# Loads of u, v and z that wait for a matmul of PE, and an earlier turn of u of group 3, in a fused gated-attention and maxout kernel

## The chip, the cores and the metric

The kernel runs on one core of a Trainium2 chip. The metric is the device time of one execution in microseconds. Five engines work side by side, each with an instruction queue of its own: PE (matrix multiplications), DVE and ACT (elementwise work), POOL and SP (in this kernel almost only issuers of DMA transfers; POOL also does a few copies at the start). An instruction that has to wait holds up everything behind it in its own queue[...]. The transfers that they issue share 16 DMA engines.

## The reference

Eight sequences of 3072 rows. For each one a gate over squared-ReLU attention is computed, and its rows then go through a maxout feed-forward:

```python
scores = (1.0 / S) * np.matmul(z, z.transpose(0, 2, 1))   # z: 8 x 3072 x 64
attn = np.maximum(scores, 0.0) ** 2
x = (u * np.matmul(attn, v)).reshape(B * S, D)            # u, v: 8 x 3072 x 256
g = np.maximum(x @ w1, x @ w2)                            # w1, w2: 256 x 1024
out = g @ w_out                                           # w_out: 1024 x 256
```

Inputs and output are float32 in memory; the kernel multiplies in bfloat16.

## The kernel before

**Tiling.** A sequence (batch b) has 24 tiles of 128 rows. Four tiles make a group (6 per batch, g = 0 to 5), eight tiles a piece (3 per batch), two groups a couple (3 per batch, c = 0 to 2). A block A(g, blk) holds the squared scores between two groups as 128 x 2048 bfloat16; 28 such blocks are at hand and are handed round. The scores are symmetric, so about half of the blocks are computed (`score_pair`: two matmuls into PSUM at L220, ReLU on ACT at L233 into r_sb, of which there are three, and the square on DVE at L239 or L241). The others are transposes of these, made by a DMA transpose on SP (`mirror`, L272; the blocks on the diagonal are filled up by small transposes at L244). mirror(b, g, blk) gives A(blk, g).

**Stages.** Batch 0's first four groups are worked one after the other (i = 0 to 3, slots with the tile number n; matmuls at L288). From there on the loop over couples runs (i = 2 is couple (0,2), i = 3 is (1,0), and so on to i = 23). A couple has a list of steps, each with two matmuls on half of PE's rows (L905). Couple (0,2) is "plain", with 96 steps; the others multiply by a Strassen-like scheme with 84 steps, for which DVE makes sums and differences of blocks (`prepare`: L340, L344, L348, and L797 in the couple) and of v (`combine_v`: L174 to L177). Score pairs of blocks that are wanted later are spread between the steps. After a couple's steps comes `second`, the feed-forward of the couple before it: two calls of `ff` (L450, L464, L473), with the outputs copied by ACT (L485) and written out by DMAs that POOL issues (L486). While PE is in `second`, DVE works through a list of tasks for the next couple: the gates (`gate`, L434: attention output times turned u), the combinations of v, the sums and differences.

**Loads.** POOL issues the loads of u, v and z, which turn float32 into bfloat16 on the way. `load_u` (L190) fetches one group of u in two transfers of 128 KB (of bfloat16); there are two buffers, and a buffer is free when `turn_u` has read it. `turn_u` (L196) is a DMA transpose on SP that gives uT, also two buffers, read by the gates. `load_z` (L136) fetches a piece of z; `turn_z` copies it twice on DVE (L143) and transposes it on SP (L144) into zT, from which the score pairs read. `load_v` (L160) fetches a piece of v or a part of it; there are five buffers.

**What sets the order.** The order of each queue is written out by hand. In the couples, `plan` lists (step, what to do): at that step of the loop the instruction is put into its engine's queue. For a DMA on POOL this is a place in POOL's queue only: when POOL gets there, the transfer leaves as soon as its buffer is free, whatever step PE is at. In batch 0, SP's queue has around group 3 (i = 3): mirrors (0,3,4) and (0,0,5) at n = 0; mirror (0,1,5) and then `turn_z(1, 1)` at n = 4; mirror (0,3,5) at n = 8; `turn_u(0, 3)` at n = 13; `turn_z(1, 2)` at n = 17; then u of groups 4 and 5 at steps 1 and 4 of couple (0,2). POOL's queue has the load of u of group 3 at n = 1, then the first feed-forward's outputs (group 0), loads of u of groups 4 and 5, group 1's outputs, and then the v loads of couple (0,2). The gates of group 3 are the first DVE tasks of the feed-forward that follows.

In the plain couple (0,2) pieces of v are taken in the order 2, 1, 0. The second of them begins at step 32 with A(5,2) and takes A(5,3), which mirror (0,3,5) makes, from step 36 on. Its seventh score pair, at step 27, is the first that reads the z tiles of `turn_z(1, 1)`. At the end of the last couple of a batch, `load_v(b + 1, 0)` is put into POOL's queue (the buffer is that of v piece 2 of batch b); `combine_v` of that piece is the third of three in DVE's list.

The lines that the change turns on, apart from those in the diff:

```python
if b and b + 1 < B and c == 2:
    load_v(b + 1, 0)
if i + 1 < len(couples):
    forms, tasks = prepared(i + 1, gates)
```

Of the kernel before, what the change touches and what calls it, by code (L numbers as in the profile page):

```python
# [11 lines left out]
def kernel(  # L12
# [10 lines left out]
    nc = tc.nc  # L23
# [12 lines left out]
    G = 4  # L36
# [7 lines left out]
    AFTER = mybir.DependencyInfo(mybir.DependencyClass.Sync, mybir.DependencyReason.DATA)  # L44
# [23 lines left out]
    def by_tile(x):  # L68
        return x.rearrange("(p t) d -> p t d", t=NT)
# [29 lines left out]

    zT = zpool.tile([P, 4 * 2 * G, P], bf16, name="zT", bufs=1)
    zn, zd, z_first = {}, {}, []

# [27 lines left out]
    def load_z(b, piece, held=False):  # L132
        zn[b, piece] = zpool.tile([P, 2 * G, dqk], bf16, name="zn")
        if held:
            nc.vector.memset(zn[b, piece][:, 0, 0:1], 0.0)
        nc.gpsimd.dma_start(  # L136
            out=zn[b, piece], in_=by_tile(z[b])[:, ds(piece * 2 * G, 2 * G), :]
        )

    def turn_z(b, piece):  # L140
        t = zpool.tile([P, 2 * G, 2, dqk], bf16, name="zd")
# [10 lines left out]
    def load_v(b, piece, lo=0, n=2 * G, held=False):  # L152
        if (b, piece) not in vp:
            vp[b, piece] = vpool.tile([P, 2 * G, D], bf16, name="v_sb")
        t = vp[b, piece]
        if held:
            nc.vector.memset(t[:, lo, 0:1], 0.0)
        step = 2 if b > 1 else n
        for k in range(lo, lo + n, step):
            nc.gpsimd.dma_start(  # L160
                out=t[:, ds(k, step), :], in_=by_tile(v[b])[:, ds(piece * 2 * G + k, step), :]
            )

    def v_at(b, t, dc):
        return vp[b, t // (2 * G)][:, t % (2 * G), ts(dc, P)]
# [16 lines left out]
    un, uT = {}, {}  # L182

    def load_u(b, g, held=False):
        un[b, g] = unat.tile([P, G, D], bf16, name="un")
        if held:
            nc.vector.memset(un[b, g][:, 0, 0:1], 0.0)
        step = 2 if b or g > 1 else G
        for k in range(0, G, step):
            nc.gpsimd.dma_start(  # L190
                out=un[b, g][:, ds(k, step), :], in_=by_tile(u[b])[:, ds(g * G + k, step), :]
            )

    def turn_u(b, g):
        t = upool.tile([P, G, KD, P], bf16, name="uT")
# [368 lines left out]
    with tc.manual_schedule():  # L564
# [49 lines left out]
        for i in range(PLAIN):  # L614
            b, g = groups[i]
            if i:
                acc = new_acc()
            new, slots = {}, pair_slots(i)
            for slot, (n, dc) in enumerate(steps_of(i)):
                tick += 1  # L620
                k = need(b, g, n)
                upto = max(k, min(done + 1, k + AHEAD)) if slot in slots else k
                while done < min(upto, len(pairs)):
                    emit_pair()
                if i == 0 and slot in (10, 22):
                    zT_pe(12 if slot == 10 else 20, 8 if slot == 10 else 4, "act")
                    if slot == 22:
                        for x in z_first:
                            x.release()
                attn_unit(b, g, n, acc, dc, n == 0, n == NT - 1)  # L630
                if n == NT - 1 and i < PLAIN - 1:
                    if i < 2:
                        new[dc] = drain_fast(acc, dc)
                    else:
                        new.update(drain(acc, [dc]))
                if dc:
                    continue
                if i in (1, 2) and n in (5, 8):
                    k = n // 8
                    nc.vector.tensor_add(sums[k][0], *sums[k])  # L640
                    sums[k] = sums[k][0]
                first = 17 if i == 3 else 11
                if i and n == first:
                    gates = gate(*groups[i - 1], sums)
                if i and n in (first, first + 3):
                    gates.pop(0)()
                if i == 0 and n == 14:
                    turn_u(0, 0)
                if (i, n) in ((1, 8), (2, 1), (3, 1)):
                    load_u(0, i, held=True)  # L650
                if i and n == (0, 16, 14, 13)[i]:
                    turn_u(0, i)
                if (i, n) in ((0, 18), (2, 12)):
                    w_in = ((w2_sb, moe_w2), (w1_sb, moe_w1)) if i == 0 else ((w_out_sb, moe_w_out),)
                    nc.vector.memset(w_in[0][0][:, 0, 0:1], 0.0)
                    for w_sb, w in w_in:
                        nc.gpsimd.dma_start(
                            out=w_sb, in_=w.rearrange("(c p) f -> p c f", p=P)
                        )
                if later and n % 4 == 0 and (i == 3 or i and n > 12):  # L660
                    later.sort(key=lambda block: block[2])
                    mirror(*later.pop(0))
                if i == 2 and n == 16:
                    nc.vector.tensor_sub(w15_sb, w1_sb, w2_sb)  # L664
                    w1.release()
                    w2.release(after=COOL)
                if (i, n) == (2, 15):
                    nc.sync.dma_start_transpose(
                        w2T.ap.rearrange("p (k r) -> p k r", r=P), w2.ap
                    )  # L670
                if (i, n) in ((1, 16), (2, 14)):
                    load_z(1, i - 1, held=True)
                if (i, n) in ((2, 17), (3, 4)):
                    turn_z(1, i - 2)
                if (i, n) == (3, 5):
                    load_z(1, 2, held=True)
                if (i, n) == (3, 17):
                    turn_z(1, 2)
            sums = new
# [65 lines left out]
        b, g = groups[PLAIN - 1]  # L745
# [9 lines left out]
        for i in range(PLAIN // 2, len(couples)):  # L755
            b, c = couples[i]
# [3 lines left out]
                b, c, forms, supers=PLAIN_COUPLES.get(i)  # L760
# [78 lines left out]
            plan = [(1, turn_u, b, q1), (4, turn_u, b, q2)]  # L839
            if i + 1 < len(couples):  # L840
                nb, nc_ = couples[i + 1]
                plan += [(70, load_u, nb, 2 * nc_), (76, load_u, nb, 2 * nc_ + 1)]
            if b + 1 < B:
                plan += (
                    [
                        (8, load_z, b + 1, 0),
                        (14, load_z, b + 1, 1),
                        (44, turn_z, b + 1, 0),
                        (58, turn_z, b + 1, 1),
                    ],  # L850
                    [(8, load_z, b + 1, 2), (44, turn_z, b + 1, 2), (45, load_v, b + 1, 2)],
                    [(10, load_v, b + 1, 1)],
                )[c]
            if i == 2:
                plan = [
                    (1, turn_u, 0, 4),
                    (4, turn_u, 0, 5),
                    *((17 + 8 * k, load_v, 1, (1, 2, 0)[k // 2], k % 2 * G, G) for k in range(6)),
                ]
            if i == 3:  # L860
                plan = [
                    (2, load_u, 1, 0),
                    (6, load_u, 1, 1),
                    (14, load_z, 2, 0),
                    (18, load_z, 2, 1),
                    (22, turn_u, 1, 0),
                    (26, turn_u, 1, 1),
                    (66, turn_z, 2, 0),
                    (len(steps), load_u, 1, 2),
                    (len(steps), load_u, 1, 3),  # L870
                ]
# [11 lines left out]
            for s, pair in enumerate(steps):  # L883
                while halves_done and halves_done[0][0] <= s:
                    _, name, mm = halves_done.pop(0)
# [13 lines left out]
                for half, (name, w, blk, j) in enumerate(pair):  # L899
                    rows = ds(half * R, R)  # L900
                    if name not in acc:
                        acc[name] = acc_tile((PLAIN_BANK if plain else BANK)[name])
                    a = blk()
                    left[name] -= 1
                    mm = nc.tensor.matmul(  # L905
                        a.out(acc[name]),
                        w()[rows],
                        a.moving(rows, j),
                        start=name not in opened,
                        stop=left[name] == 0,  # L910
                    )
                    opened[name] = True
                    if (s, half) in marks:
                        halves_done.append((s + (2 if plain else G), marks[s, half], mm))
                    if (s, half) in waits:
                        relay = relays[waits[s, half]]
                        tc.add_manual_dep(mm.ins, relay.ins.name, AFTER, reason="half done")
                    a.quota -= 1
                    if not a.quota:
                        a.release()  # L920
# [48 lines left out]
```

## Time and profile before

| what | value |
|---|---|
| median of 14 runs | 916.36 us |
| lowest, highest | 914.9, 921.52 us |
| the profiled execution: its time, its span | 914.9 us, 913.1 us |
| mean granted TensorE clock | 0.998 |
| share of the span in the chain that ended last | PE 96%, DVE 1%, ACT 1%, the rest under 1% each |
| DMA: SP's queue (transposes for the most part) | 359040 packets, 91.79 MB, 62.6% of 16 engines' span |
| DMA: POOL's queue (loads and outputs) | 37424 packets, 52.58 MB, 32.1% |
| POOL idle ahead of outputs (L486), for ACT's copies | 535.1 us, 86 times |
| POOL idle ahead of loads of u (L190), for turns of u | 89.6 us, 13 times |
| POOL idle ahead of loads of v (L160), for matmuls | 27.2 us, 7 times |

How to read it. The span is one execution, from the first to the last instruction; the 1.8 us between it and the execution's time lie around it. In the chain of waits the profile goes back from the last instruction, at each step to what released it; an engine with 96% of that chain has the work that sets the end. Idle time of POOL and SP says nothing by itself: they wait by design. In the timelines, a line gives start and duration in us, engine, line, operation, what is written and read, the count, and in brackets the idle time just before and what ended it. "SPq" marks SP's issuing of DMAs; its duration is the issue, not the transfer.

### The profile page before, as it was taken

The numbers are of one execution on the slowest core, as the hardware profiler recorded it, in microseconds if no ns is written. First come the engines' busy times: TensorE is split into PE (matmuls) and PEld (weight loads), VectorE is DVE, ScalarE is ACT, GpSimd is POOL, SyncE is SP. The second block draws the span as 40 slices with busy tenths as digits, with TensorE's granted clock in tenths as the row PEclk, the third lists the DMA queues.
The fourth block names the chain that finished last, engine by engine and source line by source line (L and its number), as shares of the span: only waits on it lengthen the run. The fifth ranks groups of instructions, "written<-read, shape, count | busy, mean of one in ns | idle before, by whom it ended". The sixth has DMA issues, their size and how long they took to land.

```text
span 913.1 us, 19389 instructions
## 1 busy us (share of the span) xinstructions
PE 899.3 (98%) x7478; PEld 520.8 (57%) x7526; DVE 722.5 (79%) x1097; ACT 601.4 (66%) x1192; POOL 160.8 (18%) x303
## 2 busy tenths in 40 slices
PE   9998999999999999999999999999999999999998
PEld 4454565665565655665546656566465564655655
DVE  6753689788997799887997979979799788995640
ACT  7985967567666676667666666766766667673445
POOL 4102021211202121201213022030320212101000
PEclk9999999999999999999999999999999999999999
DMA  9999999989999997999979999898988999887201
GB/s 176 166 191 187 175 187 166 177 153 162 184 178 161 171 174 124 186 161 166 188 128 200 147 166 181 139 210 149 164 165 137 187 162 175 163 165 138 75 24 70
DMA packets 396557, 145.61 MB, mean 159 GB/s; under 512 B 361904, under 2 KB 387632, under 8 KB 396464
## 3 DMA queue, kind: packets, MB, share of 16 engines
q1 hardware_dynamic: 359040, 91.79, 62.6%
q0 software_dynamic: 37424, 52.58, 32.1%
q8 instruction: 59, 0.97, 0.4%
q14 instruction: 34, 0.28, 0.1%
HBM read 59.77 MB, written 25.17 MB: 93 GB/s over the span
## 4 chain that ended last, share of the span: by engine, by line
PE 96%; DVE 1%; issue 1%; ACT 1%; DMA 0%; ACTq 0%; SPq 0%; DVEq 0%
PE acc L905 44%; PE o_ps L473 18%; PE d_ps L450 18%; PE s_ps L220 7%; PE o_ps L464 5%; PE acc L288 4%; ACT r_sb L233 1%; DVE blk L241 0%; DMA uT<-un 0%; PE acc L592 0%; DVE xT L434 0%; PE w2o_ps L686 0%; PE tpz L125 0%; DVE w_sb L664 0%; DVE blk L239 0%
## 5 line engine op out<-in xcount | busy, mean ns | idle before, releaser
L905 PE MATMUL acc<-blk,v_sb 64*128 64x512 bf16 x2208 | 453.2, 378 | 0.0
L233 ACT ACTIVATE r_sb<-s_ps 128x512 bf16<-128x512 f32 (+3 forms) x672 | 335.3, 560 | 126.2 <-PE s_ps L220 76.3
L905 PE MATMUL acc<-blk,vt 64*128 64x512 bf16 x1512 | 364.1, 376 | 0.0
L905 PEld LDWEIGHTS <-v_sb 64*128 64x128 bf16 x2208 | 179.0, 94 | 135.0 <-issue 7.7
L241 DVE TENSOR_TENSOR blk<-r_sb 128x1024 bf16<-128x1024 bf16 x257 | 172.2, 688 | 76.2 <-ACT r_sb L233 75.5
L457 ACT ACTIVATE g_sb<-d_ps 128x512 bf16<-128x512 f32 x384 | 193.4, 629 | 29.3 <-PE acc L905 17.8
L473 PE MATMUL o_ps<-w_out_sb,g_sb 128*128 128x256 bf16 x1536 | 175.5, 273 | 0.0
L905 PEld LDWEIGHTS <-vt 64*128 64x128 bf16 x1512 | 139.2, 94 | 62.3
L450 PE MATMUL d_ps<-xT,w_sb 128*128 128x512 bf16 x720 | 167.7, 379 | 2.6 <-issue 0.2
L473 PEld LDWEIGHTS <-g_sb 128*128 128x128 bf16 x1536 | 150.3, 98 | 17.4
L485 ACT COPY o_sb<-o_ps 128x512 f32<-128x512 f32 (+1 forms) x98 | 56.4, 577 | 132.9 <-PE o_ps L473 132.9
L486 POOL DMA_DIRECT2D out_dram<-o_sb x88 | 48.1, 547 | 535.1 <-ACT o_sb L485 535.1
L220 PE MATMUL s_ps<-zT 64*128 64x512 bf16 (+3 forms) x676 | 130.4, 358 | 4.6 <-ACT r_sb L233 4.1
L782 DVE TENSOR_TENSOR h_sb<-h_sb,acc 128x512 f32<-128x512 f32 x168 | 109.4, 682 | 28.7 <-ACT h_sb L786 20.9
L450 PEld LDWEIGHTS <-w_sb 128*128 128x128 bf16 x768 | 73.2, 98 | 89.4 <-issue 9.8
L344 DVE TENSOR_TENSOR blk<-blk,blk 128x2048 bf16<-128x2048 bf16 x63 | 77.2, 1225 | 4.5 <-DMA blk<-blk 2.4
L340 DVE TENSOR_TENSOR blk<-blk,blk 128x2048 bf16<-128x2048 bf16 x63 | 76.7, 1218 | 0.0
L797 DVE TENSOR_TENSOR blk<-blk,blk 128x2048 bf16<-128x2048 bf16 x63 | 76.6, 1218 | 0.0
L434 DVE SCALAR_TENSOR_TENSOR xT<-h_sb,uT 128x512 bf16<-128x512 f32 x96 | 62.0, 684 | 17.7 <-DMA uT<-un 16.4
L348 DVE TENSOR_TENSOR blk<-blk,blk 128x2048 bf16<-128x2048 bf16 x63 | 73.3, 1218 | 0.1
L190 POOL DMA_DIRECT2D un<-in_u_dram x94 | 50.4, 558 | 107.3 <-DMA uT<-un 89.6
L239 DVE TENSOR_TENSOR blk<-r_sb 128x512 bf16<-128x512 bf16 (+3 forms) x162 | 46.5, 324 | 20.0 <-ACT r_sb L233 18.9
(49 smaller groups left out, 358.1 us busy)
## 6 DMA issues: line engine op xcount, KB each, us to landing
out_dram<-o_sb POOLq DMA_DIRECT2D x88, 256.0 KB, 3.7
un<-in_u_dram POOLq DMA_DIRECT2D x92, 128.0 KB, 5.0
v_sb<-in_v_dram POOLq DMA_DIRECT2D x74, 128.0 KB, 5.3
blk<-blk SPq DMA_TRANSPOSE x240, 4.8
v_sb<-in_v_dram POOLq DMA_DIRECT2D x11, 256.0 KB, 7.3
zn<-in_z_dram POOLq DMA_DIRECT2D x21, 128.0 KB, 4.1
out_dram<-o_sb SPq DMA_DIRECT2D x6, 256.0 KB, 2.0
blk<-in_moe_w_dram POOLq DMA_DIRECT2D x2, 512.0 KB, 6.1
```

The source lines that it names most:

```text
L220: nc.tensor.matmul(s_ps[h][:, lo[h] :], zT[rows, z_at(b, blk * G + tiles[h]), :], zT[rows, q + lo[h] // P : q + G, :].rearrange("p t c -> ...
L233: nc.scalar.activation(o, s, AF.Relu)
L241: nc.vector.tensor_mul(a[:, k : k + 2, :], r, r)
L340: nc.vector.tensor_add(*alike(f["S1"], f["A21"], f["A22"]))
L344: nc.vector.tensor_sub(*alike(f["S2"], f["S1"], f["A11"]))
L348: nc.vector.tensor_sub(*alike(f["S3"], f["A11"], f["A21"]))
L450: nc.tensor.matmul(d_ps, w15_sb[:, kc, ts(nb, P)], xT[:, kc, :], start=(kc == 0), stop=(kc == KD - 1),)
L457: nc.scalar.activation(g_sb[:, nb, :], d_ps, AF.Relu)
L473: nc.tensor.matmul(o_ps[t // 2][:, t % 2, :], g_sb[:, nb, ts(t, P)], w_out_sb[:, nb, :], start=False, stop=(nb == KF - 1 and t % 2 == 1),)
L782: nc.vector.tensor_add(out, a, b_)
L797: nc.vector.tensor_sub(f["A12"].ap, f["A12"].ap, f["S2"].ap)
L905: mm = nc.tensor.matmul(a.out(acc[name]), w()[rows], a.moving(rows, j), start=name not in opened, stop=left[name] == 0,)
```

## The change

Every load of u, v and z in the loop over couples now waits for the matmul that stands last in PE's queue at the place where the load is put into POOL's queue (`pace` holds it; it is empty before the first couple, so that earlier loads don't wait). The places in `plan` are spread more widely, and loads of a whole piece of v are split in two. `turn_u(0, 3)` moves from n = 13 to n = 3 in group 3, that is, ahead of mirror (0,1,5), `turn_z(1, 1)` and mirror (0,3,5) in SP's queue. The load of v piece 0 after a batch's last couple keeps its place in the code, and waits there for that couple's last matmul.

```diff
--- before.py
+++ after.py
@@ -99,6 +99,15 @@
 
 
 
+    pace = []
+
+    def load(tile_, source):
+        dma = nc.gpsimd.dma_start(out=tile_, in_=source)
+        if pace:
+            tc.add_manual_dep(dma.ins, pace[-1].ins.name, AFTER, reason="paced")
+
+
+
     zT = zpool.tile([P, 4 * 2 * G, P], bf16, name="zT", bufs=1)
     zn, zd, z_first = {}, {}, []
 
@@ -133,9 +142,7 @@
         zn[b, piece] = zpool.tile([P, 2 * G, dqk], bf16, name="zn")
         if held:
             nc.vector.memset(zn[b, piece][:, 0, 0:1], 0.0)
-        nc.gpsimd.dma_start(
-            out=zn[b, piece], in_=by_tile(z[b])[:, ds(piece * 2 * G, 2 * G), :]
-        )
+        load(zn[b, piece], by_tile(z[b])[:, ds(piece * 2 * G, 2 * G), :])
 
     def turn_z(b, piece):
         t = zpool.tile([P, 2 * G, 2, dqk], bf16, name="zd")
@@ -157,9 +164,7 @@
             nc.vector.memset(t[:, lo, 0:1], 0.0)
         step = 2 if b > 1 else n
         for k in range(lo, lo + n, step):
-            nc.gpsimd.dma_start(
-                out=t[:, ds(k, step), :], in_=by_tile(v[b])[:, ds(piece * 2 * G + k, step), :]
-            )
+            load(t[:, ds(k, step), :], by_tile(v[b])[:, ds(piece * 2 * G + k, step), :])
 
     def v_at(b, t, dc):
         return vp[b, t // (2 * G)][:, t % (2 * G), ts(dc, P)]
@@ -187,9 +192,7 @@
             nc.vector.memset(un[b, g][:, 0, 0:1], 0.0)
         step = 2 if b or g > 1 else G
         for k in range(0, G, step):
-            nc.gpsimd.dma_start(
-                out=un[b, g][:, ds(k, step), :], in_=by_tile(u[b])[:, ds(g * G + k, step), :]
-            )
+            load(un[b, g][:, ds(k, step), :], by_tile(u[b])[:, ds(g * G + k, step), :])
 
     def turn_u(b, g):
         t = upool.tile([P, G, KD, P], bf16, name="uT")
@@ -648,7 +651,7 @@
                     turn_u(0, 0)
                 if (i, n) in ((1, 8), (2, 1), (3, 1)):
                     load_u(0, i, held=True)
-                if i and n == (0, 16, 14, 13)[i]:
+                if i and n == (0, 16, 14, 3)[i]:
                     turn_u(0, i)
                 if (i, n) in ((0, 18), (2, 12)):
                     w_in = ((w2_sb, moe_w2), (w1_sb, moe_w1)) if i == 0 else ((w_out_sb, moe_w_out),)
@@ -839,32 +842,37 @@
             plan = [(1, turn_u, b, q1), (4, turn_u, b, q2)]
             if i + 1 < len(couples):
                 nb, nc_ = couples[i + 1]
-                plan += [(70, load_u, nb, 2 * nc_), (76, load_u, nb, 2 * nc_ + 1)]
+                plan += [(60, load_u, nb, 2 * nc_), (78, load_u, nb, 2 * nc_ + 1)]
             if b + 1 < B:
                 plan += (
                     [
                         (8, load_z, b + 1, 0),
-                        (14, load_z, b + 1, 1),
+                        (26, load_z, b + 1, 1),
                         (44, turn_z, b + 1, 0),
                         (58, turn_z, b + 1, 1),
                     ],
-                    [(8, load_z, b + 1, 2), (44, turn_z, b + 1, 2), (45, load_v, b + 1, 2)],
-                    [(10, load_v, b + 1, 1)],
+                    [
+                        (8, load_z, b + 1, 2),
+                        (44, turn_z, b + 1, 2),
+                        (24, load_v, b + 1, 2, 0, G),
+                        (42, load_v, b + 1, 2, G, G),
+                    ],
+                    [(14, load_v, b + 1, 1, 0, G), (36, load_v, b + 1, 1, G, G)],
                 )[c]
             if i == 2:
                 plan = [
                     (1, turn_u, 0, 4),
                     (4, turn_u, 0, 5),
-                    *((17 + 8 * k, load_v, 1, (1, 2, 0)[k // 2], k % 2 * G, G) for k in range(6)),
+                    *((14 + 12 * k, load_v, 1, (1, 2, 0)[k // 2], k % 2 * G, G) for k in range(6)),
                 ]
             if i == 3:
                 plan = [
                     (2, load_u, 1, 0),
-                    (6, load_u, 1, 1),
-                    (14, load_z, 2, 0),
-                    (18, load_z, 2, 1),
-                    (22, turn_u, 1, 0),
-                    (26, turn_u, 1, 1),
+                    (12, load_u, 1, 1),
+                    (26, load_z, 2, 0),
+                    (40, load_z, 2, 1),
+                    (24, turn_u, 1, 0),
+                    (32, turn_u, 1, 1),
                     (66, turn_z, 2, 0),
                     (len(steps), load_u, 1, 2),
                     (len(steps), load_u, 1, 3),
@@ -910,6 +918,7 @@
                         stop=left[name] == 0,
                     )
                     opened[name] = True
+                    pace[:] = [mm]
                     if (s, half) in marks:
                         halves_done.append((s + (2 if plain else G), marks[s, half], mm))
                     if (s, half) in waits:
```

## The prediction

> **What bounds the kernel now.** I read the page first, then the chain of waits in order of time, then the table by stage, then the timelines of PE, DVE, SP and POOL around the one place that stood out.
>
> ```profile
> PE 899.3 (98%) x7478; PEld 520.8 (57%) x7526; DVE 722.5 (79%) x1097; ACT 601.4 (66%) x1192; POOL 160.8 (18%) x303
> ```
>
> PE is busy 98% of the span. Is that real work? The chain lists the first feed-forward stretch after the middle couple of each batch:
>
> ```profile
> 405.15 3.19 PE d_ps L450 x14
> ...
> 515.30 3.19 PE d_ps L450 x14
> ...
> 625.44 3.19 PE d_ps L450 x14
> ```
>
> The distance is 110.14 to 110.15 us every time. It can be counted: on PE's timeline four steps of a couple (8 matmuls) take 0.86 us, so a step is 0.2155 us, and a score pair costs the same. A batch has 3 x 84 steps (54.3 us), 42 pairs (9.05 us) and six feed-forwards of 7.8 us (46.8 us): 110.15 us. From batch 2 to 6 PE never waits, so no load order can win anything there; it can only lose. The place that does wait is the first couple, (0,2), from 79.3 to 111.3 us. By the same count its 96 steps and 22 pairs need 25.4 us; it takes 32.0. That is 6.6 us lost:
>
> ```profile
> 80.00:84.00 4.00, 4.00 (x40) 1.77 (x38) 0.00 (x0) 3.24 (x6) 0.00 (x0) 1.00 1.22 246
> 84.00:88.00 4.00, 1.48 (x14) 0.58 (x11) 1.05 (x2) 0.00 (x0) 0.61 (x2) 1.00 1.00 191
> 88.00:92.00 4.00, 2.29 (x13) 0.97 (x14) 3.44 (x6) 3.04 (x6) 3.69 (x7) 0.80 0.96 150
> 92.00:96.00 4.00, 4.00 (x32) 1.99 (x30) 2.08 (x3) 2.72 (x6) 1.06 (x2) 0.77 1.09 242
> ```
>
> The columns are window, PE, PEld, DVE, ACT, POOL, granted clock, DMA share, GB/s. DVE does nothing from 80 to 84, PE stops inside 84 to 92, and for 8 us the clock is only 0.80 and 0.77, which costs 4 x 0.20 + 4 x 0.23 = 1.7 us. DVE and PE say why:
>
> ```profile
> 86.95 1.29 DVE L434 SCALAR_TENSOR_TENSOR xT<-h_sb,uT 128x512 bf16<-128x512 f32 x2 [14.92 <-DMA uT<-un]
> ```
> ```profile
> 89.60 0.86 PE L220 MATMUL s_ps<-zT 64*128 64x512 bf16 x2 [4.11 <-ACT r_sb L233]
> ```
>
> DVE sits 14.92 us in the gate of group 3 because its turned u is late; the squares behind it don't run, ACT has no r_sb, PE no PSUM, and PE idles 4.11 us. With the 1.7 us of clock this is 5.8 of the 6.6. SP shows why u is late:
>
> ```profile
> 72.73 6.48 SPq L272 DMA_TRANSPOSE blk<-blk  x1
> ```
> ```profile
> 79.32 1.53 SPq L144 DMA_TRANSPOSE zT<-zd  x1
> 80.95 2.47 SPq L272 DMA_TRANSPOSE blk<-blk  x1
> 83.52 1.28 SPq L196 DMA_TRANSPOSE uT<-un  x1
> ```
>
> SP has run transposes back to back since 35 us and is some 25 us behind PE; u of group 3 (83.52) stands behind three of them. Their landings, issue plus time to land, are 82.0 (mirror (0,1,5)), 83.0 (z piece 1), 85.3 (mirror (0,3,5)), 86.8 (u): undisturbed, 2.4 us for a mirror and some 1.2 for z or u.
>
> **What the Trainium skill says.** "TensorE: Matmul & The Clock Gate", section "What's actually happening": PE falls to half clock after an idle window of about 3.4 us and needs as long to come back. The trace agrees: one idle of 4.11 us, one slow stretch. "DMA: Bandwidth & Descriptors", section "Queues, rings and completion order": each DMA engine takes turns between queues packet by packet. The page's section 3 fits a bias: 359040 packets for 91.79 MB on SP's queue are 256 B each, 37424 for 52.58 MB on POOL's are 1405 B, so beside a burst of loads the transposes get the smaller part. Measured: the u transpose issued at 92.50, amid six v loads, took 15.1 us to land against 3.3 for the one at 83.52.
>
> **The change part by part.**
>
> *Turning u of group 3 at n = 3 instead of 13.* By the code, SP's order becomes u, mirror (0,1,5), z, mirror (0,3,5): u is issued at 72.73, its rows having landed by 56.9 and its buffer (group 1's) having been read by 45.5. The transpose ahead of it lands at 76.8 (70.33 + 6.5). Then comes the stretch in which two outputs and u of group 4 (0.79 MB, issued 70.7 to 73.5) hold the DMAs until 80, so u lands at about 80.5, not 86.8. DVE's gates (1.29 us) end by 82, about when the couple's first r_sb is there (81.2), and r_sb has three buffers: this stall goes, with its slow clock. Removed: 6.6 us at most.
>
> What is late next: all that u passes moves 1.2 us back, to 84.2 for z and 86.6 for mirror (0,3,5). Without the stall PE wants z at step 27, for the seventh pair (79.3 + 33 x 0.2155 = 86.4), and A(5,3) from that mirror at step 36 (88.8). Alone this fits, by 2.2 us each. But POOL's queue moves too:
>
> ```profile
> 87.39 1.07 POOL L190 DMA_DIRECT2D un<-in_u_dram  x2 [13.31 <-DMA uT<-un]
> 88.43 1.12 POOL L486 DMA_DIRECT2D out_dram<-o_sb  x2
> 89.51 2.18 POOL L160 DMA_DIRECT2D v_sb<-in_v_dram  x4
> ```
>
> Load u of group 5 waited for that turn, with two outputs and the v loads queued behind. Now the load and outputs go at 81, v at steps 14 (83) and 26 (86): 1.31 MB beside these very transposes. Price: the 0.79 MB at 70.7 stretched two mirrors from 2.4 to 4.5 and 5.2 us, 4.9 us or 6.2 us per MB. All of it ahead would be 8.1 us, half 4.1. From 83 on I take half for the mirror: 86.6 + 4.1 = 90.7, up to 93, against 88.8: a new stall of 1.9 to 4.3 us, as an estimate 2.5, short enough to keep the clock. Bounds: 0 if the transposes hold their turn, 6.1 if the whole burst goes first and the clock falls again. So 6.6 - 2.5 = 4.1 us won here, 0.5 to 6.6.
>
> *The wait on a matmul.* POOL runs nothing in a couple but loads, and outputs come after all of them in its order; no output waits behind a paced load. An already passed semaphore costs POOL nothing that PE sees, and I price the matmuls' signals at nothing (bounds 0 and 1 us overall). The covers: u at steps 60 and 78 is turned in the next couple, 16 us of feed-forward later; z at 8 and 26 is copied at 44 and 58, 32 steps or 8 us later; v pieces 2 and 1 at 24/42 and 14/36 are combined 13 us or more later. Against that, v lands in 5.6 us at the median and 12.3 at worst, u in 5.0 and 10.9. Cost nothing; if cover goes, DVE waits first. Couple (0,2)'s own v loads end at step 74, some 20 us before their use.
>
> *v piece 0 of the next batch, after the couple.* This one gets later:
>
> ```profile
> 329.99 2.11 POOL L160 DMA_DIRECT2D v_sb<-in_v_dram  x4 [4.61 <-PE acc L905]
> ```
> ```profile
> 342.13 0.42 DVE L174 TENSOR_TENSOR vt<-v_sb 128x512 bf16<-128x512 bf16 x1
> ...
> 348.63 3.49 DVE L348 TENSOR_TENSOR blk<-blk,blk 128x2048 bf16<-128x2048 bf16 x3
> ```
> ```profile
> 352.13 0.38 PE L905 MATMUL acc<-blk,vt 64*128 64x512 bf16 x1
> ```
>
> It left when its buffer's last matmul was done, 2.1 us before the couple's last; now it waits for that last one (332.1). DVE's third combine reads it at 342.13, and from there DVE runs without a gap into the differences that end at 352.12, while PE takes the last of them at 352.13. DVE has no slack here. The fourth load is issued at 333.7 and may take 8.4 us; at these boundaries it took 4 to 5 us, 7.5 once. Cost nothing; beyond 8.4 us each us is paid on PE, at six boundaries.
>
> Sum: 913.1 - 4.1 = 909.0 us of span, plus the 1.8 us around it (914.9 - 913.1) = 910.8 for the profiled run. The median stands 1.46 above that run: 912.3.
>
> **The rivals.** *All 6.6 us come:* the transposes keep their turn in 83 to 89. For it: alone they have 2.2 us of slack; against: the 15.1 us landing. 916.36 - 6.6 = 909.8. *Moved, not removed:* PE stands at step 27 or 36 for some 4 us and falls to half clock again, in all 6 us; the change then doesn't do what it is for. For it: work for the DMAs is unchanged and their share is above 1 until 116 us. 915.9, between 914.5 and 917. *Slower, by v piece 0:* with u of step 78 just ahead of it in POOL's queue it takes 10 us to land; DVE is late by 1.6 to 1.7 us, and so is PE, six times, 10.2 us. It decides from 8.4 us of landing. Against: only the first boundary came near. 916.36 - 4.1 + 10.2 = 922.5.
>
> **How the numbers follow.** Forecast (910.5 to 914.5) 0.45, all of it 0.19, moved 0.20, slower 0.16. A run of this kernel can be told from no change at about 0.2%, 1.8 us: faster is below 914.5, slower above 918.2. Faster: 0.19 and nearly all of 0.45, less a tail: 0.61. Same: the moved case and that tail, 0.22. Slower: 0.17. The range, 909.0 to 917.2, takes the first three cases and leaves the last one and the tails out.
>
> **What would show it.** Right: u of group 3 issued on SP near 72.7 and landing near 80; DVE's 14.92 us wait down to about 8; couple (0,2) taking 27 to 29 us, with a PE wait of 1 to 4 us on z or a mirror at its step 27 or 36 and no clock of 0.8; batches still 110.15 us apart. Wrong: u landing after 84, a second slow clock, or a batch period above 110.5 us with DVE waiting at L174.

## The result, and the profile after

The changed kernel takes 934.1 us at the median of 10 runs (923.3 to 938.42), the kernel before 916.67 (48 runs, 912.91 to 924.7). The ratio on record is 1.0151, 95% interval 1.0124 to 1.0179; the medians alone are 1.9% apart. The ratios of this document leave out slow executions, more than 1.5% above the quickest of their kernel: here three of eleven (one execution more than the median counts), in e3 below nine of twelve, so that e3's ratio of 1.0000 describes three executions only. The changed kernel is slower by 1.5% or a little more, where 912.3 us was forecast. The profiled execution took 938.42 us (span 936.6) and lies at the upper end of these runs; a second profile of the same kernel (e9 below) took 930.77.

The page, first its busy times, then the chain that ended last by engine:

```profile
PE 904.8 (97%) x7478; PEld 521.1 (56%) x7526; DVE 723.1 (77%) x1097; ACT 600.5 (64%) x1192; POOL 160.4 (17%) x303
...
PE 84%; DMA 8%; DVE 3%; issue 2%; POOL 1%; ACT 0%; ACTq 0%; DVEq 0%; POOLq 0%
```

PE is busy 5.5 us longer with the same 7478 instructions. The slow clock of couple (0,2) explains only some 0.2 us of that (3.8 us at half clock, as read below, against 3.4 before); the rest is not explained here. And 8% of the chain is transfers. The chain in order of time shows which:

```profile
83.00 17.82 DMA blk<-blk
...
192.43 3.19 PE d_ps L453 x14
...
236.16 11.32 DMA out_dram<-o_sb
...
304.84 3.19 PE d_ps L453 x14
...
343.36 11.56 DMA v_sb<-in_v_dram
...
418.07 3.19 PE d_ps L453 x14
...
532.30 3.19 PE d_ps L453 x14
...
799.22 12.89 DMA out_dram<-o_sb
```

The batches, 110.14 us apart before, are now 112.41, 113.23 and 114.23 us apart (304.84 - 192.43, 418.07 - 304.84, 532.30 - 418.07). To see where within a batch, I took the length of each couple from PE's timeline, from its first matmul to the feed-forward that follows:

```
couple           (0,2)   first couple of batches 2, 3, 4, 5, 6, 7     other couples
before           32.02   20.94 20.94 20.94 20.94 20.94 20.94          18.46 to 21.26
after            39.55   23.11 23.94 24.93 23.75 20.94 24.53          at most 0.10 longer
after, again     38.30   22.40 22.89 23.09 22.30 22.03 22.04          at most 0.10 longer
```

So there are two places, and they make up the whole. Couple (0,2) got 7.5 us longer instead of 4.1 shorter; the first couples got 15.6 us longer together, and the second couples 0.5 us: 23.6, against 936.6 - 913.1 = 23.5 us of span. In the second profile: 6.3 + 9.1 + 0.5 = 15.9 against 15.9.

**Couple (0,2).** DVE's and PE's timelines, with the idle time before an instruction and its releaser in brackets:

```profile
82.01 1.29 DVE L437 SCALAR_TENSOR_TENSOR xT<-h_sb,uT 128x512 bf16<-128x512 f32 x2 [10.75 <-DMA uT<-un]
```
```profile
86.99 0.39 PE L223 MATMUL s_ps<-zT 64*128 64x512 bf16 x2 [0.61 <-DMA zT<-zd]
...
100.87 1.89 PE L913 MATMUL acc<-blk,v_sb 64*128 64x512 bf16 x8 [11.11 <-DMA blk<-blk]
```

The old stall, DVE in the gate until 86.95, is gone: the gate runs at 82.01. In its place PE stands at step 27 for z (0.61 us) and at step 36 for the mirror (0,3,5), 11.11 us. That mirror was issued at 83.00 and landed 17.82 us later, which is the first line of the chain. The table by stage (columns as before: window, PE, PEld, DVE, ACT, POOL, clock, DMA share, GB/s):

```profile
84.00:88.00 4.00, 3.39 (x32) 1.50 (x30) 3.19 (x5) 3.63 (x8) 1.68 (x4) 1.00 0.94 126
88.00:92.00 4.00, 1.76 (x18) 0.68 (x13) 2.07 (x3) 2.67 (x6) 0.00 (x0) 1.00 1.18 203
92.00:96.00 4.00, 0.00 (x0) 0.00 (x0) 0.00 (x0) 0.00 (x0) 0.00 (x0) 0.80 1.27 110
96.00:100.00 4.00, 0.00 (x0) 0.00 (x0) 0.00 (x0) 0.00 (x0) 0.00 (x0) 0.50 1.35 67
100.00:104.00 4.00, 3.13 (x16) 1.37 (x17) 0.00 (x0) 0.81 (x2) 0.53 (x1) 0.50 1.15 207
104.00:108.00 4.00, 4.00 (x38) 1.93 (x34) 1.88 (x3) 2.98 (x7) 0.53 (x1) 0.92 1.21 122
```

No engine does anything from 92 to 100, while transfers issued by 88 are still under way: the DMAs move 110 and 67 GB/s at shares of 1.27 and 1.35. So work of the engines is not what holds these transfers up. Section "What's actually happening" of "TensorE: Matmul & The Clock Gate" in the Trainium skill has the clock fall in such an idle window and need as long as that window (about 3.4 us) to recover. Here PE starts at 100.87 at 0.50 and is back at full clock some 0.6 us into the window that begins at 104 (0.08 x 4 us at half clock): 3.8 us, which agrees.

**The boundaries.** The waits of the whole execution, as total us, times, longest us:

```profile
DVE vt L179 <- DMA v_sb<-in_v_dram: 15.9, 5, 4.1
...
PE acc L913 <- DMA blk<-blk: 11.1, 1, 11.1
...
ACT o_sb L488 <- DMA out_dram<-o_sb: 22.5, 5, 5.5
```

DVE waits five times for v piece 0 at L179, as the rival "slower" had it; its total of 15.9 us is close to the 15.6 us that the five first couples lost. ACT waits as often for outputs to leave a buffer, and at two of the five boundaries the chain runs through such an output and not through v (236.16 and 799.22 above): outputs are late there together with v. The v loads at one boundary, as the list of loads in 453 to 459 us shows them:

```profile
L105 POOL DMA_DIRECT2D v_sb<-in_v_dram x4: 528/542/558, 455.0 to 456.6; - x4
L105 POOL DMA_DIRECT2D un<-in_u_dram x2: 528/532/536, 453.5 to 454.0; - x2
...
DMA to landing us min/median/max: 3.0/8.3/12.7
```

u of step 78 is issued 1 us ahead of the four v loads, and the last of these takes 12.7 us to land; before, at the same boundary, the four took 3.3 to 4.8 us, and the last u load had left 4.2 us ahead of them.

### The profile page after: what moved, and what is told of

Read it like the earlier page. It is cut to its first block, busy times and chain, and to the rows that moved or that the text cites. A ratio compares the mean times of both kernels' runs of the same rounds, so it can differ in the third digit from the quotient of the medians.

```text
span 936.6 us, 19409 instructions
## 1 busy us (share of the span) xinstructions
PE 904.8 (97%) x7478; PEld 521.1 (56%) x7526; DVE 723.1 (77%) x1097; ACT 600.5 (64%) x1192; POOL 160.4 (17%) x303
## 3 DMA queue, kind: packets, MB, share of 16 engines
q1 hardware_dynamic: 359040, 91.79, 64.7%
## 4 chain that ended last, share of the span: by engine, by line
PE 84%; DMA 8%; DVE 3%; issue 2%; POOL 1%; ACT 0%; ACTq 0%; DVEq 0%; POOLq 0%
PE acc L913 42%; PE o_ps L476 14%; PE d_ps L453 14%; PE s_ps L223 7%; DMA v_sb<-in_v_dram 4%; PE o_ps L467 4%; PE acc L291 3%; DMA out_dram<-o_sb 3%; DMA blk<-blk 2%; POOL v_sb L105 1%; DVE blk L343 1%; DVE blk L347 0%; DVE blk L351 0%; DVE blk L244 0%; PE acc L595 0%
## 5 line engine op out<-in xcount | busy, mean ns | idle before, releaser
L913 PE MATMUL acc<-blk,v_sb 64*128 64x512 bf16 x2208 | 455.7, 378 | 11.1 <-DMA blk<-blk 11.1
L437 DVE SCALAR_TENSOR_TENSOR xT<-h_sb,uT 128x512 bf16<-128x512 f32 x96 | 62.0, 684 | 13.5 <-DMA uT<-un 12.2
L105 POOL DMA_DIRECT2D v_sb<-in_v_dram x85 | 45.5, 543 | 113.2 <-PE acc L913 107.2
```

The source lines that it names most:

```text
L105: dma = nc.gpsimd.dma_start(out=tile_, in_=source)
L913: mm = nc.tensor.matmul(a.out(acc[name]), w()[rows], a.moving(rows, j), start=name not in opened, stop=left[name] == 0,)
```

## The experiments

**e1: only the turn.** The first question is which half of the change owns which place. TURN says that couple (0,2) belongs to the earlier turn, with the loads of before.

```diff
-                if i and n == (0, 16, 14, 13)[i]:      # kernel before
+                if i and n == (0, 16, 14, 3)[i]:
                     turn_u(0, i)
```

> Only the turn of u of group 3 moves to n = 3; loads and their places are those of before. Theory TURN (the moved turn lets u of group 5 and two outputs into the DMAs while mirror (0,3,5) is on its way, and all v loads right after them): PE stands at step 36 of couple (0,2) for 8 us or more, with a slow clock after it, and the couple takes 36 to 42 us against 32.0 before and 40 in the changed kernel; batches stay 110.15 us apart; 918 to 926 us in all. Theory PACED V (the stall comes from the v loads being held back to steps 14 and 26): no stall at step 36, couple (0,2) takes 25 to 28 us, 910 to 913 us.

Measured: 926.99 us (4 runs), ratio 1.0114 (1.0081 to 1.0146). Couple (0,2) takes 43.52 us and everything after it is as before, batches 110.14 us apart. PE's wait for the mirror:

```profile
PE acc L905 <- DMA blk<-blk: 15.6, 1, 15.6
```
```profile
83.88 21.87 DMA blk<-blk
```

So the stall at step 36 needs none of the pacing. With v loads left as early as buffers allow, it is longer than in the changed kernel (11.1): the mirror landed 21.9 us after its issue.

**e2: only the pacing.** The changed kernel with the turn at n = 13.

```diff
-                if i and n == (0, 16, 14, 3)[i]:      # changed kernel
+                if i and n == (0, 16, 14, 13)[i]:
                     turn_u(0, i)
```

> The changed kernel with the turn of u of group 3 back at n = 13. Theory TURN: couple (0,2) is as before, DVE waits some 15 us for u, PE 4 us, 32 us in all, and no 11 us wait for a mirror; batches 112 to 114 us apart as in the changed kernel; 922 to 930 us. Theory PACED V: a wait for the mirror of 8 us or more beside the one for u, couple (0,2) takes 38 us or more, 930 us or more.

Measured: 924.21 us (8 runs), ratio 1.0082 (1.0047 to 1.0116). Couple (0,2) takes 32.80 us, with the old stall in the gate, and the first couples take 21.3 to 23.1 us:

```profile
DVE xT L437 <- DMA uT<-un: 17.9, 2, 16.4
...
DVE vt L179 <- DMA v_sb<-in_v_dram: 7.9, 6, 2.2
```

The boundaries belong to the pacing, and the two halves cost separately: 1.1% and 0.8%.

**e3: v piece 0 free again.** WAIT says that v piece 0 is late because it waits for the couple's last matmul; QUEUE says that it is late because of u of step 78 beside it.

```diff
-        if pace:                                   # changed kernel, load()
+        if pace and not free:
...
-                load_v(b + 1, 0)
+                load_v(b + 1, 0, free=True)
```

> The changed kernel, but the load of v piece 0 at a batch's end waits for no matmul. Theory WAIT (this wait is what makes it late): it leaves 2 us earlier, lands before DVE asks for it, batches are 110.15 us apart again, 12 to 15 us are won. Theory QUEUE (u of step 78, which waits for a matmul 6 steps before the end, stands ahead of it in POOL's queue): it leaves only some 0.5 us earlier, DVE still waits at L179, batches stay 112 us or more apart, less than 4 us are won.

Measured: 930.17 us (12 runs). DVE still waits at every boundary, and the first couples still take 21.3 to 24.3 us.

```profile
DVE vt L179 <- DMA v_sb<-in_v_dram: 9.9, 6, 3.4
```

This speaks against WAIT, but weakly: behind the paced u in POOL's queue, v piece 0 left only some 0.5 us earlier. e4 is the sharper test.

The times fall into two groups: three of the 12 executions took 913.35 to 919.68 us at a granted clock of 0.999 or 1.0, the others 927 to 937 at 0.991 to 0.996. The profiled one is of the three: its couple (0,2) took 26.58 us, without the long stall. Read by the clock, then, the stall of that couple comes and goes between executions of one program. In this profile u of group 3 landed at 77.8 and the load of u of group 5, which waits for that buffer, left at 78.4; in the profile of the changed kernel these were 81.9 and 82.4. The mirror (0,3,5) landed 9.2 us after its issue instead of 17.8:

```profile
80.53 9.19 DMA blk<-blk
```

By the clock, 2 of 11 executions of the changed kernel escaped it as well (923.3 and 924.91 us, at 1.0 and 0.999).

**e4: the loads of u free again.** The counterpart: v piece 0 still waits for the last matmul, and u leaves as soon as its buffer allows.

```diff
-            load(un[b, g][:, ds(k, step), :], ...)        # changed kernel
+            load(un[b, g][:, ds(k, step), :], ..., free=True)
```

> The changed kernel, but loads of u wait for no matmul; v piece 0 still waits for the couple's last one. Theory WAIT: batches stay 112 us or more apart. Theory QUEUE: u leaves early, and v piece 0 alone, waiting for the last matmul, is later than before by 2 us and no more; if u's company was the trouble, it lands within 8 us and batches are 110.2 to 111 us apart.

Measured: 923.14 us (6 runs), ratio 1.0072 (1.0045 to 1.0098). Every first couple takes 20.94 us, and DVE has no wait for v at all. v piece 0, still paced, landed in 3.3 to 6.4 us:

```profile
L105 POOL DMA_DIRECT2D v_sb<-in_v_dram x4: 533/553/568, 228.0 to 229.5; - x4
...
DMA to landing us min/median/max: 3.3/5.6/6.4
```

So the wait on the last matmul costs nothing, and WAIT falls; the company of u costs. What is left is the couple (0,2) of 37.37 us.

**e5: u at steps 52 and 64.** All waits kept, only u's places moved away from the couple's end.

```diff
-                plan += [(60, load_u, nb, 2 * nc_), (78, load_u, nb, 2 * nc_ + 1)]
+                plan += [(52, load_u, nb, 2 * nc_), (64, load_u, nb, 2 * nc_ + 1)]
```

> The changed kernel with the loads of u at steps 52 and 64 of a couple in place of 60 and 78. Theory QUEUE (what hurts at a batch's end is the paced load of u just ahead of v piece 0, through its company in the DMAs, not through being paced): all loads stay paced and batches are still 110.2 to 111 us apart, with no wait of DVE at L179; what is left over before is couple (0,2) alone, 917 to 926 us. Rival (pacing as such spoils the batch's end): batches 112 to 114 us apart as in the changed kernel, 925 us or more.

Measured: 921.19 us (20 runs), ratio 1.0028 (1.0004 to 1.0052). All first couples are at 20.94 us; couple (0,2) keeps its stall in the profile, 40.1 us:

```profile
PE acc L913 <- DMA blk<-blk: 12.0, 1, 12.0
```

So u may be paced, if it leaves 4.5 us ahead of v piece 0 and not 1 us. Two of the 20 executions ran at full clock; they took 909.49 and 911.86 us. They have no profile; if their clock means that the stall stayed away, this is the forecast's time with quiet boundaries.

**e6: u of group 5 late.** U5 says that the early load of u of group 5, and the outputs released behind it, are what delays the mirror.

```diff
-            + [lambda g=g: load_u(0, g) for g in (4, 5)],      # changed kernel
+            + [lambda: load_u(0, 4)],
...
-                    (4, turn_u, 0, 5),
+                    (40, load_u, 0, 5),
+                    (66, turn_u, 0, 5),
```

> The changed kernel, but u of group 5 is loaded at step 40 of couple (0,2) and turned at step 66; the first two v loads stay at steps 14 and 26. Theory U5 (the load of u of group 5, let go by the earlier turn, meets mirror (0,3,5)): the wait at step 36 falls below 3 us, couple (0,2) takes 26 to 29 us, 12 to 14 us less than in the changed kernel's slow couple. Rival V OR OUTPUTS (0.5 MB of outputs and 0.5 MB of v are enough): the wait at step 36 stays above 6 us. Batches as in the changed kernel in both.

Measured: couple (0,2) takes 25.57 us, close to its floor by my count (25.4), and the mirror lands after 7.6 us. But the time is 925.86 us (9 runs), ratio 1.0097 (1.0062 to 1.0133): the next couple, (1,0), takes 32.14 us, after DVE stood 10.9 us in its gate for a turned u. The table by stage shows the crowd later on, with v's paced loads and the load of u beside the mirrors:

```profile
92.00:96.00 4.00, 4.00 (x40) 1.82 (x38) 2.54 (x4) 3.79 (x8) 1.49 (x3) 1.00 1.56 89
96.00:100.00 4.00, 4.00 (x42) 1.79 (x38) 2.32 (x4) 3.79 (x8) 0.53 (x1) 1.00 1.11 109
...
124.00:128.00 4.00, 1.25 (x10) 0.51 (x11) 3.76 (x11) 1.09 (x2) 1.08 (x2) 0.86 0.90 253
```

The DMAs move 89 and 109 GB/s at shares of 1.56 and 1.11, and PE stands in the following couple: the cost moved. For couple (0,2) this fits U5. It is one profile, and the stall stays away by itself at times, but five of the nine executions read a clock of 0.998 or more, and the profiled one, at 0.994, has its slow clock in (1,0): at least six of nine without the long stall, against two of fifteen of the changed kernel (with e9 below). The edit also lets the two outputs leave earlier, at 80.0 and 81.8, ahead of the mirror (82.6); u of group 5 and the outputs behind it are not told apart.

**e7: v's loads late too.** e6, with v from step 42 on, every 8 steps.

```diff
-                    *((14 + 12 * k, load_v, 1, ...) for k in range(6)),
+                    *((42 + 8 * k, load_v, 1, ...) for k in range(6)),
```

> As the kernel before this one in the list, and the v loads of couple (0,2) begin at step 42, so that only two outputs are beside the mirror. No wait above 1 us at step 36 under any theory that blames loads; couple (0,2) takes 25.5 to 26.5 us. Batches 112 to 114 us apart by u at step 78. 917 to 924 us. If the wait at step 36 stays, the outputs alone or the transposes ahead of it are its cause.

Measured: 926.26 us (4 runs), ratio 1.0102 (1.0068 to 1.0137). Couple (0,2) 25.57, (1,0) 24.35; but the first couples of batches 2 to 6 take 22.5 to 25.1 us, and the time misses the 917 to 924 expected. That u of step 78 was left in makes this run poor at telling the first couple's worth.

**e8: the first couple alone.** The kernel before, with the turn at n = 3, and u of group 5 and v in couple (0,2) paced as in e7; nothing else is paced.

> The kernel before with u of group 3 turned at n = 3, u of group 5 loaded at step 40 and turned at step 66, v loads of couple (0,2) paced from step 42 on; nothing else is paced, all other places as before. If the two parts are what the runs so far say, couple (0,2) takes 25.5 to 26.5 us, batches are 110.15 us apart, and 5 to 6.5 us are won on the kernel before: 910 to 912 us, ratio 0.993 to 0.995.

Measured: 918.66 us (22 runs), ratio 1.0025 (1.0007 to 1.0043). The expected 910 to 912 was missed. Couple (0,2) takes 25.58 us, 6.4 less, and the rest is as before, but couple (1,0) takes 28.03, 7.1 more: u of group 5, turned at step 66, landed at 116.6, and DVE stood in the next gate, the old stall one couple on:

```profile
116.70 1.29 DVE L437 SCALAR_TENSOR_TENSOR xT<-h_sb,uT 128x512 bf16<-128x512 f32 x2 [6.43 <-DMA uT<-un]
```

**e9: the changed kernel again**, to have a second profile.

> The changed kernel once more, beside the next two, for a second profile of it. Couple (0,2) takes 26 to 28 us in the runs where u of group 3 lands by 78 us and 37 to 41 us where it lands after 80 us; the first couples of batches 2 to 7 take 21 to 25 us each against 20.94 in the kernel before; 923 to 938 us.

Measured: 931.0 us (4 runs), ratio 1.0135 (1.0096 to 1.0174); its couples are in the table above.

```profile
PE acc L913 <- DMA blk<-blk: 10.5, 1, 10.5
...
DVE vt L179 <- DMA v_sb<-in_v_dram: 9.6, 6, 2.2
```

The same two places with the same releasers.

**e10 and e11: towards a version that wins.** e10 is e8 with u of group 5 loaded at step 34 and turned at 38, and v from step 40. e11 has the same first couple with the changed kernel's pacing everywhere else, u at steps 52 and 64.

```diff
-                    (40, load_u, 0, 5),      # e8
-                    (66, turn_u, 0, 5),
+                    (34, load_u, 0, 5),
+                    (38, turn_u, 0, 5),
```

> The kernel with only couple (0,2) paced, in which the couple after it paid 7 us because DVE waited 6.4 us for u of group 5, whose turn stood at step 66 behind a mirror that took 18 us. Here u of group 5 is loaded at step 34 and turned at step 38, ahead of mirror (1,1,2), and v comes from step 40 on. If that turn was the whole cost, couple (0,2) takes 25.6 us, couple (1,0) 20.9 to 22 us, 910 to 912 us in all. If the DMAs simply have too much to do in this couple, the wait comes back elsewhere (at v of piece 0, or at a mirror) and couple (1,0) takes 24 us or more.

> The same first couple, and from there on the changed kernel's paced loads with u at steps 52 and 64: couple (0,2) 25.6 us, (1,0) as in the kernel above, first couples of the batches 20.94 us. 910 to 913 us if the turn was the whole cost; pacing then costs and gains nothing in the batches.

Measured: e10 914.3 us (22 runs), ratio 0.9962 (0.9938 to 0.9986); e11 914.13 us (22 runs), ratio 0.9955 (0.9933 to 0.9978). Both beat the kernel before by 0.4%, and their medians lie 2% below the changed kernel's. Couple (0,2) is 25.57 us in both profiles, and (1,0) still takes 26.97 and 25.33 instead of 20.94: most of what is won comes back there. So both miss the 910 to 912 and 910 to 913 expected, and the turn of u of group 5 was not the whole cost: in e10 DVE now waits in (1,0) for a mirror.

```profile
DVE blk L800 <- DMA blk<-blk: 4.9, 1, 4.9
```

In e11 one first couple takes 21.96 us, so its pacing is nearly but not quite free. Its couple (0,2) is a useful check on e3: u of group 3 landed at 81.8, as late as in the changed kernel, and the mirror still landed after 5.0 us. The quickest five executions of e10 took 908.0 to 909.9 us.

**e12: only the v loads late.** In couple (0,2) u of group 5 and the outputs go early as in the changed kernel; only the v loads move (the diff of e7).

> Couple (0,2) keeps the early load of u of group 5 and the two outputs at 82 to 84, and gives up only the two v loads of its steps 14 and 26 (they go from step 42 on, every 8). SHARE theory (my prediction's pricing: each MB beside the mirror costs it time in proportion): with 0.5 of 1.3 MB gone, the mirror (0,3,5) is some 40% less late, it lands by about 93 to 95 and PE waits 3 to 6 us instead of 11.1. U5 theory (the early load of u and the outputs that follow it are what delays the mirror, the v loads merely come late too): PE waits 9 us or more as before. V theory (the two v loads are what delays it): the mirror lands within 8 us, PE waits 2 us or less and couple (0,2) takes under 28 us. In all three the first couples of batches 2 to 7 stay at 22 to 25 us, so that the time is 917 to 932 us.

Measured: 920.84 us (20 runs), ratio 1.0045 (1.0018 to 1.0071). The first couples are slow (21.9 to 22.7 us) as expected, and couple (0,2) takes 25.57 us without a wait. But in this profile u of group 3 had landed at 77.1 and u of group 5 left at 77.6, so it is one in which the stall may have stayed away by itself. The clock of the 20 executions says more: 19 are at 0.996 or above and one at 0.993, where 9 of 11 of the changed kernel are at 0.991 to 0.995. So, by the clock, the two v loads are needed for the long stall, and U5 alone says too much; by e6 an early u of group 5, with the outputs behind it, is needed too. SHARE is not ruled out: eleven of the 20 read 0.996 to 0.998, as most executions of the kernel before do with its shorter stall, and the one profile is of an execution at 1.0.

## Why the prediction was wrong

**Right: the stall that goes, and the places of what comes.** Turned first, u of group 3 was issued at 71.8 (predicted 72.7) and landed at 81.9 (80.5), DVE's wait fell from 14.92 to 10.75 us (to about 8, I had said), and the old stall went. z at step 27, which was to fit by 2.2 us, was nearly in time: PE waited 0.61 us. The next to be late is A(5,3) at step 36. Of the loads only v piece 0 got a wait of weight; the covers of the others held. That nearly all of the 6.6 us can be had in this couple is shown by e6, e7, e8, e10 and e11, where it takes 25.57 or 25.58 us.

**Wrong, first step: the size of the new stall.** "a new stall of 1.9 to 4.3 us, as an estimate 2.5, short enough to keep the clock." It is 11.1 us (10.5 in the second profile), 0.6 at step 27, and 2.3 more (39.55 - 25.57 - 11.11 - 0.61), of which the 3.8 us at half clock are 1.9. The rival "moved, not removed" had the place and the second slow clock, got 0.20, and priced it at 6 us. The term that failed is the price of 1.31 MB beside the mirror: 6.2 us per MB, half of it ahead, at worst all of it, 8.1 us. The mirror was planned for 86.6 and landed at 100.83, 14.2 us late, more than if all of the burst had gone first. (The worst case was summed wrongly as well: 86.6 + 8.1 - 88.8 is a wait of 5.9 us, and with 1.7 us of slow clock 7.6, not 6.1; the part would then lose 1.0 us instead of winning 0.5.) The price assumed that the DMAs keep their throughput and only share it out. They did not, and the profile before had shown it: in 100 to 104 us of the same couple, behind the v loads, they moved 97 GB/s at a share of 1.23, and the mirror issued at 93.94 took 16.9 us.

```profile
100.00:104.00 4.00, 4.00 (x40) 2.14 (x38) 2.77 (x4) 3.79 (x8) 0.00 (x0) 1.00 1.23 97
```

There nothing waited for that mirror. I took the price from the milder stretch at 70.7, and used the 15.1 us of the u transpose only as a sign of who goes first. After the change, the two queues in 92 to 100 us, as packets, MB and the time of their packets as a share of 16 engines:

```profile
q1 hardware_dynamic: 1235, 0.31, 84.8%
q0 software_dynamic: 202, 0.37, 43.1%
```

A transpose's packet took 0.848 x 8 us x 16 / 1235 = 88 ns. Over the whole execution it is 0.647 x 936.6 x 16 / 359040 = 27 ns. The section "Queues, rings and completion order" of "DMA: Bandwidth & Descriptors" in the Trainium skill has the engines take turns between queues packet by packet; from that I argued who gets the smaller part, but it doesn't say that a transpose's packet takes three times as long. Nor is it shown that the packets of the profile, 256 B each, are the packets of that section, which hold several descriptors. Which property of the crowd makes packets slow, no run here isolates: e7, e8, e10 and e11 show that taking u of group 5 and v away is enough for this couple, e6 and e12, with the reserve made there, that one of the two may be. e3, with the same transfers, u of group 5 and the outputs some 4 us earlier, moved 168 to 286 GB/s in the windows of 80 to 96 us, so the bytes alone don't make the crowd slow.

**Wrong, second step: v piece 0.** "Cost nothing; beyond 8.4 us each us is paid on PE, at six boundaries." The threshold was right. The longest landing at the six boundaries was 10.8, 11.6, 12.7, 11.5, 8.4 and 12.2 us; less 8.4 this gives 2.4, 3.2, 4.3, 3.1, 0 and 3.8, and the first couples lost 2.2, 3.0, 4.0, 2.8, 0 and 3.6. The wrong term was the landing: I took the 4 to 5 us of the kernel before, where the last u load had left 4 to 5 us ahead of v, for a boundary at which the change puts u 1 us ahead of it. (The boundary where it took 7.5 us is the one with u nearest, 3.9 us.) The rival "slower" named this mechanism and place, got 0.16, and priced it at 10 us of landing; e4 and e5, in which first couples take 20.94 us again, show that it is the right one and that the wait itself is free. In 232 to 248 us of the changed kernel, across such a boundary:

```profile
q1 hardware_dynamic: 4652, 1.17, 88.5%
q0 software_dynamic: 657, 0.97, 41.9%
```

and in e4, 230 to 246 us, with u out of the way:

```profile
q1 hardware_dynamic: 6272, 1.57, 52.0%
q0 software_dynamic: 814, 1.48, 37.3%
```

In e4 both queues move more bytes in less packet time: a transpose's packet takes 21 ns there and 49 in the changed kernel (share x 16 us x 16 / packets).

**The sum.** Both failed steps leaned the same way: the gain of 4.1 us became a loss of 7.5, and nothing at the boundaries became 15.6 us (9.1 in the second profile). The forecast's own sign of failure, "a batch period above 110.5 us with DVE waiting at L174" (L179 after), is what came.

## What to carry to other kernels

Where transfers are near their limit, don't price a moved load by its megabytes alone: look for what it will run beside, and search the profile before for the worst stretch with such company, also where nothing waited for it. Here the mirror came 14.2 us late, against 4.1 priced by bytes. A landing time read before a change holds only for the neighbours that the transfer had then; check it again wherever the change puts another transfer within a few us ahead of it. And a stall taken from one couple must be followed into the next: here e6, e8 and e10 won 6.4 us in couple (0,2) and paid 11.2, 7.1 and 6.0 us in (1,0).

## What was not expected of the hardware

- One transpose of 4.4 us took 17.8 us (21.9 in e1) beside loads and outputs, with the DMAs' share at 1.27 to 1.35 and 67 to 110 GB/s moved. At a like share of 1.22 to 1.23, windows of the same couple before moved anything from 97 to 246 GB/s: the share alone doesn't tell how much is moved.
- A shift of a few us goes with the long stall. In all twelve profiles with the earlier turn, the mirror (0,3,5) took 17.8 us or more in the five where both of group 1's outputs were issued 0.4 to 1.1 us after it (after, e1, e4, e5, e9), and 9.2 us or less in the seven where both were issued at least 0.4 us ahead of it. u of group 3 alone doesn't sort them: it landed at 80.4 to 82.7 in the five, but at 81.8 in e11. No run moves the outputs alone, so their order is a sign and not a cause that is shown.
- A single profile doesn't tell which outcome is the rule. By the granted clock of each run, 0.999 or 1.0 in two of the fifteen executions of the changed kernel and 0.991 to 0.995 in thirteen, the stall is the rule; both profiled executions of it, at 0.995 and 0.994, have the stall, while the case without is seen only in profiles of other versions (e3 at 1.0).
